# Last-row products in two column halves, activations held to the end of a slot, and projection pieces spread out, in a fused attention and MLP kernel

## The chip, the cores and the metric

The kernel runs on one core of one Trainium2 chip. The metric is the device time of one execution in microseconds (us), as the median of several runs of the same program. The kernel before took 1686.95 us (three runs, 1683.77 to 1687.59). The profiled execution has a span of 1682.0 us from its first to its last instruction, and the traces below count from the start of that span.

A core has five engines that run side by side and meet through semaphores: TensorE (PE in the profile; PEld is its loading of weights), VectorE (DVE), ScalarE (ACT), GpSimd (POOL) and SyncE (SP), which here only issues transfers.

## The reference

Attention that keeps the 32 largest scores of every row, and then a two-layer perceptron with an exact gelu:

```python
# q, k, v: (8 batches, 8 heads, 576 rows, 64), float32
scores = (q @ k.T) / sqrt(64)
kth    = 32nd largest of each row of scores
scores = where(scores >= kth, scores, -1e9)
attn   = exp(scores - rowmax) / (sum + 1e-9)
x      = (attn @ v), heads side by side       # (4608, 512)
out    = gelu(x @ w_in) @ w_out               # (512, 2048), (2048, 512)
```

Everything is float32. TensorE takes each float32 product in two passes, so that the trace has two matmul records for each product in the source; a transpose takes one.

## The kernel before

A batch has 576 rows: 4 blocks of 128 rows (`SM` = 512) and 64 last rows (`TL` = 64). Heads go in pairs. The work is cut into 144 **items**: 128 of them are one block of 128 rows for two heads, and 16 gather the last 64 rows of four heads (two pairs) into one block of 128. A loop over **slots** n issues, for different items, each stage of the attention, and fills in **pieces** of the perceptron. Tile scheduling is manual: every engine runs its instructions in the order in which this program issues them.

```python
for n in range(ahead):                       # one slot
    left[0] = 7 if START < n < START + 2 * NP else 8     # pieces in this slot; START = 10
    weights_add(unit_in(n))
    scores(n + 2)                            # PE, then two ACT copies
    product = attend(n - 3)                  # PE: attn @ v, then ACT copies to xT
    late = n > START + 1
    mlp(1)                                   # one piece: 0.86 us of PE
    tr = transposes(n - 2)                   # [tails, main(0), main(1)]
    ...                                      # (cut: where the next piece needs this product)
    softmax(n - 1, 0)                        # ACT: Prelu, Exp
    mlp(1)
    if not late:
        softmax(n - 1, 1)
    mlp(1)
    for piece in tr[:-1]:
        piece(); ready[0] = n_tok[0]; mlp(1)
    ready[0] = n_tok[0]
    if late:
        softmax(n - 1, 1)
    add_small(n - 1)                         # POOL: den
    for piece in tr[-1:] + prep_in.pop(n, []):   # prep: q and k of a later pair, transposed
        piece(); mlp(1)
    mlp(left[0])
    if n < N:
        top_k(n, {3: lambda: inverse(n - 1)})    # DVE
    threshold(n)                             # POOL
    normalise(n - 1)                         # POOL: two multiplications
    ...                                      # (cut: weights, loads)
```

The product with v for a block of 128 rows (two blocks together, 256 columns) and for last rows:

```python
o = ps.tile([P, 512], f32, tag="tp", name="o")
if t < NM:                                   # 128-row items: a head in each column half
    for j in range(NJ):                      # NJ = 5 blocks of keys
        for e in range(2):
            nc.tensor.matmul(o[e * D : (e + 1) * D, 0:n], lhsT=vt[:, j, e, :],          # L448
                             rhs=pt[:, e * NM + j if j < NM else 2 * NM, :], ...)
    nc.scalar.copy(out=xT[:, at, c], in_=o[:, 0:n])                                     # L453
else:                                        # last rows: both heads of v at once
    for r in range(2):
        vt = raw_of("v", pair + r)
        for j in range(NJ):
            nc.tensor.matmul(o[:, r * P : (r + 1) * P],                                 # L458
                             lhsT=vt[:, j].rearrange("p e d -> p (e d)"),
                             rhs=pt[:, r, j, :], ...)
    for e in range(2):
        r = slice(e * D, (e + 1) * D)
        nc.scalar.copy(out=xT[r, at : at + 2, c], in_=halves(o[r, 0 : 2 * P], e, P))    # L464
```

In the last-row form, 128 columns of v (two heads) meet 128 columns of attention (two heads). Of the four 64 x 64 blocks that come out, the two that join v of one head with the attention of the other are not used.

The scores are products of 64 x 128 parts of the array, or 64 x 64 for last rows (L294: 128 x 64 with 64 moving columns; L305: 64 x 64):

```python
nc.tensor.matmul(t_ps[half(r, e), r * TL : (r + 1) * TL],                               # L294
                 lhsT=qk[:, SM + e * TL : SM + (e + 1) * TL],
                 rhs=qk[:, SM + P + e * TL : SM + P + (e + 1) * TL], ...)
```

The PSUM tag "tp" has two buffers, which the small score tile `t_ps`, the product `o`, the transposes `tp_t` and `tp`, and the projections' transposes `tp_qk` take in turn. Each is freed by an ACT copy.

The perceptron goes in blocks of eight pieces: first layer (L496, into `h_ps`, tag "l1", two buffers), then second layer of the units before (L532). The gelu of two `h_ps` tiles is issued with the sixth piece of a second-layer block:

```python
def gelus(us):
    for u in us:
        g_of[u] = work.tile([P, nf, n], f32, tag="g", bufs=4, name="g")
        nc.scalar.activation(g_of[u], h_of.pop(u), func=AF.Gelu)                        # L507

def behind(work, x, us):                     # x = GELU_AT = 5
    need, f = work[x]
    work[x] = need, lambda: (f(), gelus(us))
    return work
```

Of the kernel before, what the change touches and what calls it, by code (L numbers as in the profile page):

```python
# [14 lines left out]
def kernel(  # L15
# [19 lines left out]
    nc = tc.nc  # L35
# [5 lines left out]
    B, H, S, D = q.shape  # L41
    P = 128
# [6 lines left out]
    TL = S - SM  # L49
    NJ = NM + 1  # L50
# [10 lines left out]
    work = ctx.enter_context(tc.tile_pool(name="work", bufs=2))  # L61
# [6 lines left out]
    xT = const.tile([P, KO, RING], f32, name="xT")  # L68
# [15 lines left out]
    def raw_of(n, pair):  # L84
        return raws[n][pair % len(raws[n])]

    def load(n, pair, queue=None, queue2=None):
        if pair >= n_pairs:
            return
        queue = queue or nc.sync  # L90
        queue2 = queue2 or queue
        b, h0 = pair // NP, 2 * (pair % NP)
        t, src = raw_of(n, pair), sources[n]
        for e in range(2):
            queue.dma_start(
                out=t[:, 0:NM, e, :], in_=src[b, h0 + e, 0:SM].rearrange("(t p) d -> p t d", p=P)
            )
            queue2.dma_start(out=t[e * TL : (e + 1) * TL, NM, e, :], in_=src[b, h0 + e, SM:S])
# [23 lines left out]
    START = 2 * NP + 2  # L122
# [60 lines left out]
    def weights_add(u):  # L183
        if u in words:
            w, _, dst = parts(u)
            d = dst.bitcast(i32)
            if on_pool(u):
                nc.gpsimd.tensor_scalar(
                    w.bitcast(i32), w.bitcast(u32), 2.0**-13, None, op0=ALU.mult
                )  # L190
            nc.gpsimd.tensor_tensor(d, d, w.bitcast(i32), op=ALU.add)
# [23 lines left out]
    def place_of(b, row):  # L215

        if row < SM:
            return b // 2 * RING + b % 2 * (SM + 2 * TL) + row
        return b // 2 * RING + SM + b % 2 * TL + row - SM
# [37 lines left out]
    def spread(t, step, n):  # L257

        return bass.AP(tensor=t.tensor, offset=t.offset, ap=[list(t.ap[0]), [step, 2], [1, n]])

    def half(r, e):


        return slice((r ^ e) * TL, ((r ^ e) + 1) * TL)

    def halves(t, e, step):

        return spread(t[:, e * TL :], step + (TL if e == 0 else -TL), TL)
# [84 lines left out]
    def inverse(i):  # L353
        if i < 0 or i >= N:
            return
        st = stat_of[i]
        nc.vector.reciprocal(st["rden"], st["den"])  # L357

    def add_small(i):
        if i < 0 or i >= N:  # L360
            return
        st = stat_of[i]
        nc.gpsimd.tensor_scalar(st["den"], st["den"], 1e-9, None, op0=ALU.add)  # L363

    def softmax(i, e):

        if i < 0 or i >= N:
            return
        st, s = stat_of[i], row(i, e)
        nc.scalar.activation(s, s, func=AF.Prelu, bias=st["neg"][:, e, 1:2], scale=1.0, alpha=STEEP)  # L370
        nc.scalar.activation(  # L371
            s, s, func=AF.Exp, bias=st["bias"][:, e : e + 1], scale=1.0,
            accum_out=st["den"][:, e : e + 1],
        )
# [55 lines left out]
    def attend(i):  # L430

        if i < 0 or i >= N:
            return False
        pair, t = items[i]
        b, at = divmod(pair, NP)
        if t < NM and t % 2 == 0:
            return False
        pt = pt_now[0]
        o = ps.tile([P, 512], f32, tag="tp", name="o")
        n, row = (2 * P, (t - 1) * P) if t < NM else (TL, SM)  # L440
        tok = place_of(b, row)
        assert read[0] >= tok + n - RING
        c = slice(tok % RING, tok % RING + n)
        if t < NM:
            vt = raw_of("v", pair)
            for j in range(NJ):
                for e in range(2):
                    nc.tensor.matmul(  # L448
                        o[e * D : (e + 1) * D, 0:n], lhsT=vt[:, j, e, :],
                        rhs=pt[:, e * NM + j if j < NM else 2 * NM, :],  # L450
                        start=(j == 0), stop=(j == NJ - 1),
                    )
            nc.scalar.copy(out=xT[:, at, c], in_=o[:, 0:n])  # L453
        else:
            for r in range(2):
                vt = raw_of("v", pair + r)
                for j in range(NJ):
                    nc.tensor.matmul(  # L458
                        o[:, r * P : (r + 1) * P], lhsT=vt[:, j].rearrange("p e d -> p (e d)"),
                        rhs=pt[:, r, j, :], start=(j == 0), stop=(j == NJ - 1),  # L460
                    )
            for e in range(2):
                r = slice(e * D, (e + 1) * D)
                nc.scalar.copy(out=xT[r, at : at + 2, c], in_=halves(o[r, 0 : 2 * P], e, P))  # L464

        if t == (NM if b % 2 == 0 else NM - 1):
            for r in range(2 if t == NM else 1):
                load("v", pair + r + NP + 1)
        if at == (NP - 1 if t < NM else NP - 2):
            assert n_tok[0] == tok  # L470
            n_tok[0] = tok + n
        return True
# [10 lines left out]
    def h_tile(u):  # L483
        if u not in h_of:
            _, n, _, nf = units[u]
            h_of[u] = ps.tile([P, nf, n], f32, tag="l1", name="h_ps")
        return h_of[u]

    def l1_piece(u, x):
        tok, n, f0, nf = units[u]  # L490
        m = 4 // nf
        i, part, c0 = x // m, x % m, tok % RING
        f = f0 + i
        assert all(2 * (f * P // WS) + r in made for r in range(2))
        for ko in range(part * KO // m, (part + 1) * KO // m):
            nc.tensor.matmul(  # L496
                h_tile(u)[:, i, :], lhsT=w_in_sb[:, ko, f * P : (f + 1) * P],
                rhs=xT[:, ko, c0 : c0 + n], start=(ko == 0), stop=(ko == KO - 1),
            )
        if f == FT - 1 and part == m - 1:  # L500
            read[0] = tok + n

    def gelus(us):
        for u in us:
            _, n, _, nf = units[u]
            g_of[u] = work.tile([P, nf, n], f32, tag="g", bufs=4, name="g")
            nc.scalar.activation(g_of[u], h_of.pop(u), func=AF.Gelu)  # L507
# [37 lines left out]
    pieces = []  # L545
    GELU_AT = 5

    def block(u, first):

        do, need = (l1_piece, units[u][0] + units[u][1]) if first else (l2_piece, 0)  # L550
        return [(need, lambda w=w, x=x: do(w, x)) for w in (u, u + 1) for x in range(4)]

    def behind(work, x, us):
        need, f = work[x]
        work[x] = need, lambda: (f(), gelus(us))
        return work

    pieces += behind(block(0, True), 7, (0, 1)) + block(2, True)
    for u in range(2, NU, 2):
# [4 lines left out]
    done = [0]  # L564

    def mlp(n):
        for _ in range(n):
            if done[0] >= len(pieces) or pieces[done[0]][0] > ready[0] or left[0] == 0:
                return
            pieces[done[0]][1]()  # L570
            done[0] += 1
            left[0] -= 1
# [32 lines left out]
    prep_in = {}  # L605
    for pair in range(2, n_pairs):
        b, p = divmod(pair, NP)
# [3 lines left out]
    for n in range(ahead):  # L611

        left[0] = 7 if START < n < START + 2 * NP else 8
        weights_add(unit_in(n))
        scores(n + 2)
        product = attend(n - 3)
        late = n > START + 1
        mlp(1)
        tr = transposes(n - 2)
        if product and n > START and done[0] < len(pieces) and pieces[done[0]][0] > ready[0]:  # L620

            for piece in tr[:1]:
                piece()
            tr, ready[0] = tr[1:], n_tok[0]
        softmax(n - 1, 0)
        mlp(1)
        if not late:
            softmax(n - 1, 1)
        mlp(1)
        for piece in tr[:-1]:  # L630
            piece()
            ready[0] = n_tok[0]
            mlp(1)
        ready[0] = n_tok[0]
        if late:
            softmax(n - 1, 1)
        add_small(n - 1)
        for piece in tr[-1:] + prep_in.pop(n, []):
            piece()
            mlp(1)  # L640
        mlp(left[0])
        if n < N:
            top_k(n, {3: lambda: inverse(n - 1)})
        else:
            inverse(n - 1)
        threshold(n)
        normalise(n - 1)

        weights_sign(unit_in(n))
        weights_size(unit_in(n + 1))  # L650
        if n >= FIRST:
            load_weights(n + 2)
        if n <= NP:
            load("v", n)

    ready[0], left[0] = NT, len(pieces)
    mlp(len(pieces))
    staging.close()


# [30 lines left out]
```

## Time and profile before

| | busy, share of the span | instructions |
|---|---|---|
| PE | 1608.8 us, 96% | 8512 |
| DVE | 1428.6 us, 85% | 3043 |
| ACT | 1189.3 us, 71% | 2147 |
| POOL | 661.9 us, 39% | 761 |

A matmul's end in the trace is modelled, and matmuls overlap, so that the busy share of PE says when it stood idle but not how fast it went. The time that a group of matmuls really takes is the distance from its first start to the start of whatever comes next on PE. ACT loads a table 136 times in all (68 ahead of gelus, 67 ahead of exponentials, one at the start), at 1283 ns each. The waits named below are those that the trace infers from semaphores: "X <- Y" says that X stood idle until Y was done.

### The profile page before, as it was taken

What the parts mean: (1) busy time and instruction counts of PE and PEld (TensorE: products, weight loads), DVE (VectorE), ACT (ScalarE), POOL (GpSimd) and SP (SyncE); (2) the same over time, 40 slices, a digit from 0 to 9 for tenths busy, and PEclk for the clock granted to TensorE, in tenths of its full rate; (3) what the DMA queues carried; (4) which work ended last, traced back from release to release, by engine and by line L of the source; (5) the groups of instructions that cost most, each with busy time, mean ns of one, the idle gap of its engine ahead of it and who ended that gap; (6) DMA issues with size and microseconds to landing.
All of it is one profiled execution on the core that took longest, in us unless ns stands there. A gap on an engine that the chain in (4) does not pass through costs nothing.

```text
span 1682.0 us, 24466 instructions
## 1 busy us (share of the span) xinstructions
PE 1608.8 (96%) x8512; PEld 1095.1 (65%) x8512; DVE 1428.6 (85%) x3043; ACT 1189.3 (71%) x2147; POOL 661.9 (39%) x761
## 2 busy tenths in 40 slices
PE   5559999999999999999999999999999999999999
PEld 4336567766666667676666667676666666766665
DVE  7998988998889888998989888898889998899900
ACT  6887767777777767777777776777777777777730
POOL 3778733333333333333333333333333333333410
PEclk7669999999999999999999999999999999999999
DMA  6422310011100111001100111001110000000000
GB/s 160 136 101 92 91 42 1 13 29 29 44 6 15 29 39 31 1 21 42 29 27 1 42 29 42 1 14 28 36 41 1 27 15 16 20 1 13 7 13 12
DMA packets 126618, 56.10 MB, mean 33 GB/s; under 512 B 117760, under 2 KB 117792, under 8 KB 126496
## 3 DMA queue, kind: packets, MB, share of 16 engines
q1 hardware_dynamic: 125376, 54.25, 11.9%
q8 instruction: 67, 1.10, 0.3%
q14 instruction: 55, 0.45, 0.1%
q10 hardware_dynamic: 1056, 0.26, 0.1%
q0 software_dynamic: 64, 0.03, 0.0%
HBM read 45.08 MB, written 9.44 MB: 32 GB/s over the span
## 4 chain that ended last, share of the span: by engine, by line
PE 88%; DVE 6%; ACT 4%; issue 1%; POOL 1%; ACTq 0%; POOLq 0%
PE h_ps L496 30%; PE y_ps L532 28%; PE o L448 8%; PE s_ps L284 7%; PE tp L417 7%; DVE top L331 3%; DVE rest L334 3%; PE o L458 2%; PE tp_qk L239 2%; PE t_ps L280 2%; PE tp_t L399 1%; PE s_ps L305 1%; ACT s L371 1%; ACT L507 1%; ACT s L370 1%
## 5 line engine op out<-in xcount | busy, mean ns | idle before, releaser
L331 DVE MAX8 top<-rest 128x8 f32<-128x576 f32 x864 | 610.4, 749 | 0.0
L496 PE MATMUL h_ps<-xT,w_in_sb 128*128 128x256 f32 (+1 forms) x2560 | 553.2, 361 | 1.6 <-ACT g L507 1.6
L532 PE MATMUL y_ps<-w_out_sb,g 128*128 128x512 f32 x1152 | 548.6, 598 | 0.0
L382 POOL TENSOR_SCALAR s<-s,rden 128x576 f32<-128x576 f32 x288 | 493.5, 1723 | 1.0 <-issue 0.7
L496 PEld LDWEIGHTS h_ps<-xT,w_in_sb 128*128 128x128 f32 x2560 | 429.4, 191 | 63.7 <-issue 18.4
L334 DVE MATCH_REPLACE8 rest<-top,rest 128x576 f32<-128x576 f32 x576 | 424.0, 745 | 0.0
L363 POOL TENSOR_SCALAR den<-den 128x2 f32<-128x2 f32 x144 | 32.0, 222 | 858.2 <-ACT s L371 857.5
L532 PEld LDWEIGHTS y_ps<-w_out_sb,g 128*128 128x128 f32 x1152 | 195.1, 190 | 166.0 <-issue 164.5
L288 ACT ACTIVATE s<-s_ps 128x1024 f32<-128x1024 f32 x128 | 131.5, 1028 | 170.1 <-PE s_ps L284 149.8
L371 ACT ACTIVATE s<-s,bias 128x576 f32<-128x576 f32 x288 | 223.3, 775 | 13.0 <-ACT s L370 0.4
L370 ACT ACTIVATE s<-s,neg 128x576 f32<-128x576 f32 x288 | 223.7, 777 | 0.8 <-POOL neg L346 0.2
L424 ACT COPY pt<-tp 128x512 f32<-128x512 f32 x256 | 147.1, 575 | 100.6 <-PE tp L417 100.1
L334 DVE MATCH_REPLACE8 rest<-top,s 128x576 f32<-128x576 f32 x288 | 212.0, 745 | 0.0
L417 PEld LDWEIGHTS tp<-ident,s 128*128 128x128 f32 x1152 | 147.8, 145 | 90.5 <-issue 57.5
L331 DVE MAX8 top<-s 128x8 f32<-128x576 f32 x288 | 202.1, 745 | 3.9 <-ACT s L289 3.9
L417 PE MATMUL tp<-ident,s 128*128 128x128 f32 x1152 | 177.7, 279 | 5.8 <-ACT pt L400 5.8
L357 DVE RECIPROCAL rden<-den 128x2 f32<-128x2 f32 x144 | 23.4, 163 | 165.4 <-POOL den L363 165.1
L448 PE MATMUL o<-pt,raw_v 128*64 128x256 f32 x1280 | 156.2, 391 | 1.8 <-ACT pt L424 1.8
L284 PE MATMUL s_ps<-qk 64*128 64x256 f32 x1024 | 152.6, 418 | 0.7 <-ACT s L288 0.7
L448 PEld LDWEIGHTS o<-pt,raw_v 128*64 128x64 f32 x1280 | 87.9, 139 | 69.5 <-issue 16.3
L284 PEld LDWEIGHTS s_ps<-qk 64*128 64x128 f32 x1024 | 92.0, 194 | 23.7 <-issue 1.8
L507 ACT ACTIVATE g<-h_ps 128x512 f32<-128x512 f32 x144 | 78.7, 595 | 39.6 <-PE h_ps L496 38.9
(63 smaller groups left out, 1110.6 us busy)
## 6 DMA issues: line engine op xcount, KB each, us to landing
raw_q<-in_q_dram SPq DMA_DIRECT2D x64, 128.0 KB, 2.3
raw_v<-in_v_dram SPq DMA_DIRECT2D x64, 128.0 KB, 2.4
out_dram<-y SPq DMA_DIRECT2D x32, 256.0 KB, 2.2
w_out_sb<-in_moe_w_in_dram SPq DMA_DIRECT2D x16, 511.8 KB, 4.8
raw_k<-in_k_dram SPq DMA_DIRECT2D x62, 128.0 KB, 2.4
w_out_sb<-in_moe_w_out_dram SPq DMA_DIRECT2D x10, 511.8 KB, 3.7
words<-in_moe_w_out_dram SPq DMA_DIRECT2D x6, 511.8 KB, 4.2
raw_q<-in_q_dram SPq DMA_DIRECT2D x64, 16.0 KB, 2.2
```

The source lines that it names most:

```text
L284: nc.tensor.matmul(s_ps[:, e, c * 256 : (c + 1) * 256], lhsT=lhsT[rows, :], rhs=qk[rows, KT + c * 256 : KT + (c + 1) * 256], start=True, s ...
L288: nc.scalar.activation(spread(s, S + TL, SM), s_ps, func=AF.Copy, scale=scale)
L331: nc.vector.max(st["top"][:, e, 8 * r : 8 * r + 8], cur[e])
L334: nc.vector.match_replace(rest[:, e], st["top"][:, e, 8 * r : 8 * r + 8], cur[e], LOWEST)
L370: nc.scalar.activation(s, s, func=AF.Prelu, bias=st["neg"][:, e, 1:2], scale=1.0, alpha=STEEP)
L371: nc.scalar.activation(s, s, func=AF.Exp, bias=st["bias"][:, e : e + 1], scale=1.0, accum_out=st["den"][:, e : e + 1],)
L382: nc.gpsimd.tensor_scalar(s, s, st["rden"][:, e : e + 1], None, op0=ALU.mult)
L417: nc.tensor.transpose(tp[:, j * P : (j + 1) * P], s[:, first + j * P : first + (j + 1) * P], ident)
L424: nc.scalar.copy(out=dst, in_=tp.rearrange("p (j n) -> p j n", j=NM))
L448: nc.tensor.matmul(o[e * D : (e + 1) * D, 0:n], lhsT=vt[:, j, e, :], rhs=pt[:, e * NM + j if j < NM else 2 * NM, :], start=(j == 0), stop= ...
L496: nc.tensor.matmul(h_tile(u)[:, i, :], lhsT=w_in_sb[:, ko, f * P : (f + 1) * P], rhs=xT[:, ko, c0 : c0 + n], start=(ko == 0), stop=(ko == ...
L532: nc.tensor.matmul(y_of[sub], lhsT=g_of[u][:, i, sub * P : (sub + 1) * P], rhs=w_out_sb[:, f, :], start=(f == 0), stop=(f == FT - 1),)
```

## The change

It has three parts.

1. **Last rows by heads.** Each product of the last rows is cut into two: v of one head (64 columns) with the attention of that head alone (64 columns), in the half of the array's columns and of the PSUM partitions that belongs to this head. The unused blocks are no longer computed, and one ACT copy moves both heads to `xT`.
2. **Gelus held.** A gelu is put on a waiting list when its piece has run, and issued at the end of the slot: after the slot's softmax, copies and preparation, ahead of the last pieces, or earlier if a first-layer block begins and needs the `h_ps` buffer. What it is for: ACT runs its work in order, and other ACT copies for which TensorE waits shall not stand behind a table load and two gelus.
3. **Preparation spread.** In a slot with two groups of preparation, the first one goes between the transposes instead of both going to the end. Besides, the later place of the second softmax half (`late`) begins one slot earlier.

```diff
@@ attend, last rows @@
                 for j in range(NJ):
-                    nc.tensor.matmul(
-                        o[:, r * P : (r + 1) * P], lhsT=vt[:, j].rearrange("p e d -> p (e d)"),
-                        rhs=pt[:, r, j, :], start=(j == 0), stop=(j == NJ - 1),
-                    )
-            for e in range(2):
-                r = slice(e * D, (e + 1) * D)
-                nc.scalar.copy(out=xT[r, at : at + 2, c], in_=halves(o[r, 0 : 2 * P], e, P))
+                    for e in range(2):
+                        nc.tensor.matmul(
+                            o[e * D : (e + 1) * D, r * TL : (r + 1) * TL], lhsT=vt[:, j, e, :],
+                            rhs=pt[:, r, j, half(r, e)], start=(j == 0), stop=(j == NJ - 1),
+                        )
+            nc.scalar.copy(
+                out=xT[:, at : at + 2, c],
+                in_=o[:, 0 : 2 * TL].rearrange("p (r n) -> p r n", r=2),
+            )
@@ l1_piece @@
+        if x == 0:
+            run_gelus()
@@ behind @@
+    waiting = []
     def behind(work, x, us):
         need, f = work[x]
-        work[x] = need, lambda: (f(), gelus(us))
+        work[x] = need, lambda: (f(), waiting.append(us))
         return work
+    def run_gelus():
+        while waiting:
+            gelus(waiting.pop(0))
@@ the loop over slots @@
-        late = n > START + 1
+        late = n > START
 ...
+        prep = prep_in.pop(n, [])
+        if len(prep) > 1 and len(tr) == 3:
+            tr, prep = tr[:1] + prep[:1] + tr[1:], prep[1:]
         for piece in tr[:-1]:
 ...
-        for piece in tr[-1:] + prep_in.pop(n, []):
+        for piece in tr[-1:] + prep:
             piece()
             mlp(1)
+        run_gelus()
         mlp(left[0])
+        run_gelus()
@@ the end @@
-    mlp(len(pieces))
+    while done[0] < len(pieces):
+        mlp(1)
+        run_gelus()
```

## The prediction, made before the changed kernel ran

> **What bounds the kernel now.** I read the page first: the busy shares, and the span in 40 slices.
>
> ```profile
> PE 1608.8 (96%) x8512; PEld 1095.1 (65%) x8512; DVE 1428.6 (85%) x3043; ACT 1189.3 (71%) x2147; POOL 661.9 (39%) x761
> ...
> PE   5559999999999999999999999999999999999999
> ```
>
> PE is below nine tenths in the first three slices only, so the span falls into stages, and I asked for the busy times of each stage (columns: window, length, then PE, PEld, DVE, ACT, POOL, the granted clock, DMA share, GB/s).
>
> ```profile
> 0.00:124.00 124.00, 70.72 (x363) 48.90 (x364) 113.37 (x231) 94.33 (x154) 71.30 (x75) 0.71 0.45 133
> 124.00:210.00 86.00, 79.64 (x434) 52.79 (x433) 79.42 (x162) 68.71 (x116) 69.78 (x49) 0.98 0.29 91
> 210.00:1596.00 1386.00, 1376.15 (x7411) 941.04 (x7412) 1235.68 (x2651) 1008.32 (x1848) 513.44 (x633) 1.00 0.09 22
> 1596.00:1682.00 86.00, 82.32 (x312) 52.33 (x308) 0.17 (x1) 17.92 (x32) 7.34 (x7) 1.00 0.03 13
> ```
>
> Until 124 us DVE is the bound (113.37 of 124 us), and the change hardly touches that. From 210 to 1596 us PE is busy for all but 10 us of 1386, at full clock; the last 86 us are the perceptron alone, again on PE. So whatever shortens PE's own work or its waits after 124 us shortens the time one for one, as long as nothing else takes over. Then the waits of PE in the steady stage (engine, line, what it waited for: us in total, times, longest):
>
> ```profile
> PE t_ps L280 <- ACT qk L243: 3.8, 3, 1.3
> PE t_ps L294 <- ACT qk L243: 2.5, 3, 0.8
> PE o L448 <- ACT pt L424: 1.8, 1, 1.8
> PE t_ps L280 <- ACT pt L424: 1.2, 1, 1.2
> PE tp_t L404 <- POOL s L382: 0.4, 1, 0.4
> ```
>
> All but the last name an ACT copy. The timeline of ACT ahead of one of them shows why the copy was late (start, duration, instruction):
>
> ```profile
> 455.47 0.56 ACT L424 COPY pt<-tp 128x512 f32<-128x512 f32 x1
> 456.04 1.28 ACT L507 ACT_TABLE_LOAD   x1
> 457.34 1.08 ACT L507 ACTIVATE g<-h_ps 128x512 f32<-128x512 f32 x2
> 458.31 0.59 ACT L243 COPY qk<-tp_qk 128x512 f32<-128x512 f32 x1
> ```
>
> The copy of qk stands behind 2.3 us of table load and gelus; PE's next scores start at 458.95, as soon as it is done. What a group of matmuls takes I read as the distance between starts on PE's timeline:
>
> ```profile
> 167.52 0.45 PE L294 MATMUL t_ps<-qk 128*64 128x64 f32 x8
> 167.90 1.09 PE L305 MATMUL s_ps<-qk 64*64 64x512 f32 x8
> ...
> 229.53 2.50 PE L458 MATMUL o<-ptt,raw_v 128*128 128x128 f32 x20
> 231.86 1.02 PE L532 MATMUL y_ps<-w_out_sb,g 128*128 128x512 f32 x2
> ...
> 898.16 2.38 PE L448 MATMUL o<-pt,raw_v 128*64 128x256 f32 x20
> 900.47 0.70 PE L496 MATMUL h_ps<-xT,w_in_sb 128*128 128x256 f32 x2
> ```
>
> A last-row product takes 231.86 - 229.53 = 2.33 us now, and its single records start 111.5 ns apart. L448 does 20 passes of 256 columns in 2.31 us, where 20 full-width passes of 256 columns, as L496 has them, start 216 ns apart and would take 4.32: its two column halves run at the same time.
>
> [...] records of L448 start in pairs 7 ns apart, a pair every 216 ns. [...] from the last pair of L448 to the first L496 it takes 103 ns more than a pair, and the first L496 pass takes 320 instead of 216 ns, together 0.2 us. [...]
>
> **Part 1, last rows by heads.** An item has 2 pairs x 5 blocks x 2 passes = 20 passes of 128 columns, and afterwards 40 of 64 columns on half the array. L294 has exactly that shape (128 rows, 64 weight columns, 64 moving columns): its records start in pairs, a pair every 58 ns, after a first pair of 107 ns. So 20 pairs take 20 x 58 = 1.16 us, plus 0.05 for the first. New is a change of mode on leaving, since now the perceptron follows directly at full width and before it the product was at full width too: 0.2 us, as after L448. The change on entering exists already. Sum 1.16 + 0.05 + 0.2 = 1.42 us (rounded), against 2.33: **0.91 us less for each of 16 items, 14.5 us**, all of it after 210 us, where PE is the bound. The ACT copies go from 32 of 259 ns to 16 of about the same: 4 us less on ACT, which lies beside other work.
>
> **Part 2, gelus held, steady stage.** In the changed order of ACT the copy of qk stands ahead of the gelus in every slot that has both. The six waits of t_ps for qk should go: 3.8 + 2.5 us idle, and about 0.16 us each that the modelled ends of matmuls hide, 1.0 in all. Besides, about 17 products of L448 start some 0.06 us late behind the same copies: 1.0. Together **8.3 us**. What it may cost: gelus end later. In a slot with preparation they start when qk is copied, about 0.9 us before the slot's end by my adding up of eight pieces at 0.86 us, scores of 1.5 and transposes, and so end about 1.5 us into the next slot, just as the next scores (1.5 us of PE) become ready for ACT. The h_ps buffers are needed there only after scores and product, 3.9 us in. So I expect no new wait in the steady stage. The number of table loads stays: gelus were already one batch in a slot.
>
> **Parts 2 and 3 in the ramp (124 to 225 us).** Here slots are short of ready work, and the places shift, in four slots. Slot 11: the copy of tails stood behind both halves of the softmax, and PE waited 2.3 us for it; with the second half later it is 0.97 + 0.78 us earlier: 1.7 gained. Slot 15: gelus now come after tails and preparation, so the first-layer block that waits for h_ps (1.6 us now) starts about 0.8 later, and the second transposes' copy, behind a softmax, comes later too, while a wait of 0.7 us for the second preparation group goes: 1.2 lost. Slot 17: gelus move from the middle to the end, so the main copies come 2.4 us earlier and the waits of 1.2 and 1.8 us at 212 and 215 us go, then 0.4: up to 3.5 gained. Sum 4.0; with normalisation on POOL close behind, I take **3.5**. The spread of preparation in the steady stage moves copies by half a us inside slots and, by the waits above, frees nothing further.
>
> **Sum.** 14.5 + 8.3 + 3.5 = 26.3 us; 1686.95 - 26.3 = 1660.6, so 1661 us, 1.5% less.
>
> **Rivals.** *The halves do not pay.* With 80 loads and matmuls in about 1.2 us, PE's issue of instructions may be the limit; L294 shows the pace for 8 passes only, not for 40. If each pass took 56 ns instead of 29, the product would stay at 2.24 us and lose 0.2 us to the mode: 16 x 0.1 = 2 us lost instead of 14.5 gained, and 1677. Against it: the pairs of L294 hold the same pace up to the last. *Another engine takes over.* DVE needs 9.7 us for an item's top-k without a wait (from 886.33 to 896.03 us), and PE's slots last 11.0 us on average (123 slots from 212 to 1567 us), those with a last-row product 11.7, afterwards 10.8. That stays above DVE, but a chain runs beside it: softmax, denominator, reciprocal after the top-k, 3.43 us of normalisation, then the tails. In one slot that I followed it had 1.3 us to spare; spreading preparation delays the second softmax by about 1.3 us. Where it runs out, a wait for normalisation replaces what was gained, a few us in all: about 1667. *The gelu's wait moves.* If ACT runs later than I count, PE waits for the score tile or for h_ps instead of qk: part 2 gives back up to 8 us, and 1669. *The ramp gives nothing,* or slot 15 costs more than I count: 1664 to 1666.
>
> **Range and chances.** The first rival would show as a whole, but is unlikely; the others are partial. On the other side the ramp may give 3 us more, if everything behind slot 11 moves up. I set 1653 to 1669. Over 2% faster would be below 1653.2: 0.08. Within 2%: 0.91. Slower by over 2%: 0.01.
>
> **What would show it.** Right: the product's line has 640 passes, and start to start an item takes about 1.4 us; no wait of t_ps for qk is left in the steady stage; PE's busy time falls by about 14 us; the last stage of 86 us is unchanged; 68 table loads ahead of gelus, give or take two. Wrong: an item near 2.2 us (issue bound); new lines of PE waiting for POOL's normalisation or for g; at 185 us a longer wait for g than 1.6 us, with more lost than the 1.2 that I set.

## The result, and the profile after

The changed kernel takes **1660.88 us** (median of four runs, 1659.89 to 1662.99) against 1686.57 of the kernel before, a ratio of 0.9852 with a 95% interval of 0.9835 to 0.9869. Runs of one kernel scatter by one to five us, so that step by step I use the profiled executions, which are 1682.0 us before and 1658.1 us after, 23.9 us apart.

The busy times of the page, and of the long stage (window, length, then PE, PEld, DVE, ACT, POOL, clock, DMA share, GB/s):

```profile
PE 1590.1 (96%) x8832; PEld 1079.1 (65%) x8832; DVE 1428.5 (86%) x3043; ACT 1182.8 (71%) x2131; POOL 661.6 (40%) x761
```

```profile
210.00:1596.00 1386.00, 1382.97 (x7859) 942.98 (x7858) 1237.16 (x2656) 1013.34 (x1851) 522.25 (x640) 1.00 0.09 22
```

PE has 320 more instructions and 19 us less busy time. In the long stage it now stands idle for 3 of 1386 us instead of 10. Its waits from 125 us on:

```profile
PE h_ps L500 <- ACT g L511: 3.7, 2, 2.6
PE tp_t L404 <- POOL s L382: 2.9, 2, 1.5
PE tp L417 <- ACT pt L400: 2.0, 2, 1.3
PE tp_t L399 <- POOL s L382: 1.1, 2, 0.6
PE t_ps L294 <- ACT pt L424: 0.9, 2, 0.6
```

The waits of t_ps for qk are gone. All that is left lies in the ramp, but for 1.2 us in the last slot. ACT's timeline at the place that was shown before the change (slot 39) has the new order:

```profile
449.58 0.56 ACT L424 COPY pt<-tp 128x512 f32<-128x512 f32 x1
450.11 0.58 ACT L243 COPY qk<-tp_qk 128x512 f32<-128x512 f32 x1
450.97 0.58 ACT L542 COPY y<-y_ps 128x512 f32<-128x512 f32 x1 [0.28 <-PE y_ps L536]
451.57 1.28 ACT L511 ACT_TABLE_LOAD   x1
```

The copy of qk follows the transposes' copy at once; PE's next scores start at 451.63, unhindered. And a last-row product on PE's timeline:

```profile
227.66 1.39 PE L459 MATMUL o<-ptt,raw_v 128*64 128x64 f32 x40
228.98 2.84 PE L536 MATMUL y_ps<-w_out_sb,g 128*128 128x512 f32 x6
```

Start to start it is 1.32 us for 40 passes, where 20 full-width passes took 2.33.

The starts of the scores bound each slot. Their distances, in us, say where the 23.9 us came from:

| | before | after | gained |
|---|---|---|---|
| start of the first scores | 9.0 | 9.4 | -0.4 |
| slot 11 | 13.13 | 9.85 | 3.3 |
| slot 14 | 11.58 | 11.99 | -0.4 |
| slot 15 | 12.45 | 15.39 | -2.9 |
| slot 16 | 11.59 | 11.78 | -0.2 |
| slots 17 and 18 | 9.03 + 15.98 | 7.64 + 14.92 | 2.4 |
| 16 slots with a last-row product | 11.68 (first of them) | 10.76 | 14.7 |
| the other slots from 23 to 140 | | | 8.8 |
| from slot 141's scores to the end | 114.6 | 116.0 | -1.45 |

### The profile page after: what moved, and what is told of

The parts are those of the page before. It is cut to its first block, busy times and chain, and to the rows that moved or that the text cites. A ratio compares the mean times of both kernels' runs of the same rounds, so it can differ in the third digit from the quotient of the medians.

```text
span 1658.1 us, 25071 instructions
## 1 busy us (share of the span) xinstructions
PE 1590.1 (96%) x8832; PEld 1079.1 (65%) x8832; DVE 1428.5 (86%) x3043; ACT 1182.8 (71%) x2131; POOL 661.6 (40%) x761
## 4 chain that ended last, share of the span: by engine, by line
PE 89%; DVE 6%; ACT 2%; POOL 1%; issue 1%; POOLq 0%; ACTq 0%
PE h_ps L500 30%; PE y_ps L536 29%; PE o L448 8%; PE s_ps L284 7%; PE tp L417 7%; DVE top L331 3%; DVE rest L334 3%; PE tp_qk L239 2%; PE t_ps L280 2%; PE o L459 1%; PE tp_t L399 1%; PE s_ps L305 1%; POOL s L382 1%; DVE w_in_sb L199 0%; ACT s L371 0%
## 5 line engine op out<-in xcount | busy, mean ns | idle before, releaser
L448 PE MATMUL o<-pt,raw_v 128*64 128x256 f32 x1280 | 155.1, 389 | 0.0
L448 PEld LDWEIGHTS o<-pt,raw_v 128*64 128x64 f32 x1280 | 87.5, 139 | 65.8 <-issue 23.9
```

## The experiments

Ten kernels ran. "Span" is that of the profiled execution. They ran in three groups, each beside the kernel before, whose median in them was 1684.45 to 1686.89 us; differences of two or three us between rows are therefore read from the spans and slots. The diffs are abridged where `...` stands.

| kernel | median us | ratio to before, 95% interval | span us |
|---|---|---|---|
| part 1 alone | 1669.31 | 0.9908, 0.9895 to 0.9921 | 1667.0 |
| part 2 alone | 1673.97 | 0.9935, 0.9923 to 0.9947 | 1672.0 |
| part 3 alone | 1693.86 | 1.0052, 1.0039 to 1.0065 | 1689.3 |
| parts 1 and 2 | 1659.56 | 0.9850, 0.9837 to 0.9864 | 1657.7 |
| changed, halves in turn | 1672.0 | 0.9915, 0.9900 to 0.9929 | 1670.3 |
| changed, a piece between | 1669.41 | 0.9898, 0.9883 to 0.9913 | 1667.7 |
| changed, one block of five | 1647.83 | 0.9772, 0.9756 to 0.9788 | 1646.3 |
| changed, with the rule | 1657.4 | 0.9833, 0.9820 to 0.9846 | 1655.4 |
| parts 1, 2, the rule | 1657.4 | 0.9838, 0.9825 to 0.9852 | 1655.0 |
| parts 1, 2, the rule, late from slot 11 | 1654.3 | 0.9819, 0.9806 to 0.9833 | 1652.9 |

**Part 1 alone.**

```diff
-                    nc.tensor.matmul(o[:, r * P : (r + 1) * P], lhsT=<both heads>, rhs=pt[:, r, j, :])
+                    for e in range(2):
+                        nc.tensor.matmul(o[e * D : (e + 1) * D, r * TL : (r + 1) * TL],
+                                         lhsT=vt[:, j, e, :], rhs=pt[:, r, j, half(r, e)])
...                                      # (cut: start and stop; the copies change as shown above)
```

> The kernel before with part 1 alone (last-row products by heads). If TensorE bounds the steady stage and nothing takes over: an item takes 1.42 us instead of 2.33, 16 items, so 14.6 us less, about 1672 us, and slots with a last-row product fall from 11.7 to 10.8 us. If another engine or the normalisation chain takes over behind it: less than 10 us gained, 1677 or more, with new waits of TensorE for POOL's normalisation.

The span fell by 15.0 us; by the medians it is 17.1. Slots with a last-row product take 10.69 to 10.80 us, as in the changed kernel, and PE's waits in the steady stage are those of before (3.8 and 2.5 us for qk). Nothing takes over: the first theory.

**Part 2 alone.**

```diff
-        work[x] = need, lambda: (f(), gelus(us))
+        work[x] = need, lambda: (f(), waiting.append(us))
...
+        run_gelus()
         mlp(left[0])
```

> The kernel before with part 2 alone (gelus held). Theory: the waits of scores for the qk copy go in the steady stage (8.3 us by the prediction, 8.8 by the changed kernel's slots), slot 17 gains about 3, slot 15 loses about 1, and the last slot loses 1.3 because its gelus now wait for the end of a second-layer block: 9.5 us in all, about 1677 us. Rival, the wait only moves to h_ps or to the score tile: under 4 us gained, 1683 or more.

The median fell by 12.4 us, the span by 10.0. From slot 23 to slot 141 it gained 8.8 us (1283.8 against 1292.6); slots 17 and 18 gained 3.4; slot 15 lost 0.3; the end lost 1.45. From 230 us to the last slot no wait of PE is left. The wait does not move: it goes.

**Part 3 alone.**

```diff
-        late = n > START + 1
+        late = n > START
+        prep = prep_in.pop(n, [])
+        if len(prep) > 1 and len(tr) == 3:
+            tr, prep = tr[:1] + prep[:1] + tr[1:], prep[1:]
```

> The kernel before with part 3 alone (preparation spread, second softmax half late one slot earlier). Theory: slot 11 gains the 3.3 us that it gained in the changed kernel, the steady stage nothing: 1683 us. Rival: the gain of slot 11 is taken back at the normalisation of the next slots, or the spread makes new waits: 1686 to 1687.

It was slower by 7.5 us, which neither expectation had. Slot 11 did gain 3.3. But from slot 23 to slot 141 the kernel took 1302.0 us instead of 1292.6, and the first line of PE's waits from 125 us on was new:

```profile
PE t_ps L294 <- ACT pt L424: 10.5, 5, 2.9
```

ACT's and PE's timelines show it (once in each odd batch, 2.93 us long in three of the four):

```profile
584.49 1.28 ACT L507 ACT_TABLE_LOAD   x1
585.78 1.09 ACT L507 ACTIVATE g<-h_ps 128x512 f32<-128x512 f32 x2
586.75 0.78 ACT L370 ACTIVATE s<-s,neg 128x576 f32<-128x576 f32 x1
587.55 1.28 ACT L371 ACT_TABLE_LOAD   x1
...
589.62 0.56 ACT L424 COPY pt<-tp 128x512 f32<-128x512 f32 x1
```

```profile
590.23 0.45 PE L294 MATMUL t_ps<-qk 128*64 128x64 f32 x8 [2.93 <-ACT pt L424]
```

A preparation group between the transposes brings the sixth piece of the second-layer block, and with it the gelus, ahead of the second half of the softmax and of the second transposes' copy. These then stand behind two table loads, and with them the buffer that the next scores need. The 9.4 us are made of three slots that take 2.1 us longer and, in the slots behind two of them, 1.6 us more at half of TensorE's clock. With gelus held no such wait is left after the ramp: part 3 is harmful without part 2.

**Parts 1 and 2 without part 3.** The edit is the two diffs above together.

> The kernel before with parts 1 and 2, without part 3. If parts 1 and 2 carry the whole gain and the spread only undoes in slot 15 what it brings in slot 11: as fast as the changed kernel or up to 1 us faster, 1660 to 1661 us, with the scores of slot 19 starting at about 225.5 us as with part 2 alone. If part 3 adds to the others (the parts alone give 17.1, 12.4 and minus 7.5 us, which sums to 22, and the whole gave 25.7): 3 us or more slower than the changed kernel, 1664 us.

It is as fast as the changed kernel (ratio 0.9850 against 0.9852). From slot 23 to slot 141 both take 1272.8 us, so that in the steady stage the spread is worth nothing. In the ramp slot 11 lacks its 3.3 us (13.11), while slot 15 takes 12.76 instead of 15.39, though PE waits 2.57 us for g there too, and slot 18 takes 13.97 instead of 14.92. Scores of slot 19 start at 225.9 us, and at 226.3 us in the changed kernel.

**Halves in turn.**

```diff
-                for j in range(NJ):
-                    for e in range(2):
+                for e in range(2):
+                    for j in range(NJ):
                         nc.tensor.matmul(o[e * D : (e + 1) * D, r * TL : (r + 1) * TL], ...)
```

> The changed kernel, but all five products of one head ahead of the five of the other, so that neighbours use the same half of the columns. Same instructions, same number of mode changes. If the gain of part 1 comes from two halves running at the same time, which needs neighbours in different halves: an item goes to about 40 x 56 ns + 0.25 = 2.5 us, 1.1 us more for each of 16 items, about 1678 us. If a 64-column pass is cheap in itself (29 ns each): no change, 1661 us.

```profile
229.88 2.01 PE L459 MATMUL o<-ptt,raw_v 128*64 128x64 f32 x40
231.81 1.55 PE L536 MATMUL y_ps<-w_out_sb,g 128*128 128x512 f32 x3
```

An item takes 1.94 us instead of 1.32, 0.62 more, and the kernel is 11.1 us slower: 10.0 in the slots with a last-row product, and most of the rest at half clock in slot 18 (16.25 us, against 14.92). So it is the overlap of two halves that pays. A step takes 58 ns in both kernels, but an item has 20 steps of two passes in the changed kernel and 31 here. The size I expected (2.5 us) was too large: 9 of the 40 records start only 3 to 6 ns after the one before, so some overlap remains although neighbours in the program use the same half. How PE comes to it I did not settle.

**A piece between.**

```diff
             for r in range(2):
                 vt = raw_of("v", pair + r)
+                if r == 1:
+                    mlp(1)
```

> The changed kernel, but with one of the slot's perceptron pieces moved between the two pairs of a last-row product, which adds a change of tiling mode in each direction and no work. If leaving the half-width mode costs 0.2 us and entering it 0.1: 0.3 us for each of 16 items, 5 us, about 1666 us. If a change of mode costs nothing and what was seen after L448 belongs to that line alone: 1661 us.

```profile
231.06 0.80 PE L461 MATMUL o<-ptt,raw_v 128*64 128x64 f32 x20
231.79 1.12 PE L538 MATMUL y_ps<-w_out_sb,g 128*128 128x512 f32 x2
232.85 0.80 PE L461 MATMUL o<-ptt,raw_v 128*64 128x64 f32 x20
233.58 1.13 PE L538 MATMUL y_ps<-w_out_sb,g 128*128 128x512 f32 x2
```

The piece takes 1.06 us between the halves, against 0.86 elsewhere, and each half 0.73. Of the first four slots with a last-row product, three are 0.35 us longer than in the changed kernel and one 0.50. A change from half width to full and back thus costs about 0.35 us, near the 0.3 expected, which makes 6 us of the 8.5 by which this kernel is slower. Most of the rest is one slot of the ramp, slot 18 (17.83 us, against 14.92), whose instructions are the same in both kernels: in this profile PE has half its clock for 6.8 us there, and in the changed kernel's not at all.

**One block of five.** This kernel leaves out four of the five blocks of keys in the last-row products, and its output lacks them.

```diff
-                for j in range(NJ):
+                for j in range(1):
...                                      # (cut: stop=(j == 0))
```

> The changed kernel with four of the five blocks of keys left out of the last-row products (the output is no longer the reference's): 8 passes instead of 40, by 4 pairs of 58 ns + 0.25 = 0.48 us an item, 0.93 less than now. If TensorE still bounds the slots with last-row products at 9.8 us: 14.9 us less, about 1646 us. If the top-k of 9.7 us with its chain through normalisation takes over before: 1652 us or more, with TensorE waiting for POOL.

The last-row slots take 9.83 us (10.03 and 9.76 for two of them), as expected for a product of 0.48 us, and PE has no wait in them. The median is 13.1 us below the changed kernel's; 14.3 of it are in the steady slots (one of each four saves 0.77 instead of 0.93), and slot 19 begins 2.5 us later, again for the clock in slot 18. So at slots of 9.8 us DVE's 9.7 us of top-k still does not take over, at least not in the four such slots that follow one another.

**With the rule.** Gelus are issued at once where the next first-layer block begins in the same slot, and in the last slot.

```diff
+    def at_once(x):
+        nxt = done[0] + 8 - x
+        fits = left[0] > 8 - x and nxt < len(pieces) and pieces[nxt][0] <= n_tok[0]
+        return fits or slot[0] >= ahead - 1
...                                      # (cut: slot[0] is set to n in the loop over slots)
-        work[x] = need, lambda: (f(), waiting.append(us))
+        work[x] = need, lambda: (f(), waiting.append(us), at_once(x) and run_gelus())
```

> The changed kernel, but gelus are issued at once where the next first-layer block begins in the same slot (that is slot 15 alone), and in the last slot. If holding the gelus is what made slot 15 take 15.4 us instead of 12.5 and the end wait 1.3 us: 4 us less than the changed kernel, about 1657 us. Rival, slot 15 lost its time to the spread preparation: only the 1.3 us of the end come back, 1659.5 us.

1657.4 us, 3.5 less. Slot 15 is back at 12.76 us, and the end at 114.6. But slot 18 grew to 16.58, so that scores of slot 19 start only 1.2 us earlier. PE waits there for normalisation as in the changed kernel (2.9 us in two waits). From this I took slot 18 to be bound by normalisation on POOL whatever comes ahead of it, and tested that with the next two.

**The rule without part 3, and with the late softmax alone.** The first is parts 1 and 2 with the rule; the second adds one line:

```diff
-        late = n > START + 1
+        late = n > START
```

> Parts 1 and 2 with the rule that issues gelus at once where the next first-layer block begins in the same slot, and in the last slot; no part 3. If slot 18 is bound by normalisation on POOL behind the top-k, what slots 11 to 17 gain before it is lost there: the same as the second version with part 3, 1657 to 1658 us, 1.4 us of it against parts 1 and 2 alone from the last slot. If the ramp adds up slot by slot: 3 us slower, 1660.5 us, for want of slot 11's gain.

> As the run before, and with the second half of the softmax late from slot 11 on, which is part 3 without the spread. If slot 18 is bound by normalisation: 1657 to 1658 us again. If the ramp adds up: 1657 us from slot 11's 3.3 us, against 1660.5 without.

They took 1657.4 and **1654.3 us**. The first number would fit the theory, the second does not, and slot 18 contradicts it in both: 13.97 and 14.00 us, although in the second it starts as early (208.5 us) as in the version with the spread, where it took 16.58. The spread makes the smaller part of this difference. In slot 16 it sends the second half of the softmax later: the denominator reaches POOL 11.4 us after the slot's start in the changed kernel (203.28 us) and 10.3 us in the last version (199.50). On POOL, behind it, stand a normalisation, a weight conversion of 5.4 us and the next normalisation back to back, for which slot 18 waits: 2.9 us with the spread; without it 1.2, and 0.9 for a copy of scores on ACT. That is 0.9 us less, as much as lies between 14.92 us in the changed kernel and 14.00 here. The other 1.7 of the 16.58 us are a stretch of 3.4 us at half clock, from 216.0 us on. The changed kernel has the same 2.9 us of waits and no such stretch; the next section shows what differs between the two. None of the four kernels that hold gelus and leave out the spread has one there, and in the last version what slot 11 gains stays to the end. It is the fastest: 6.6 us below the changed kernel by the medians, 5.2 by the spans. Two of PE's waits in it from 125 us on:

```profile
PE h_ps L500 <- ACT g L511: 1.6, 1, 1.6
PE tp_t L404 <- POOL s L382: 1.2, 1, 1.2
```

The 1.2 us of the last slot are gone, and slot 15's wait for g is 1.6 us instead of 2.6.

## Why the prediction was right, and where it was not

The predicted 1661 us is within 0.2 us of the median. By its steps:

- **PE bounds, one for one: right.** What PE was spared came back in full in the part 1 run (0.92 us in each of 16 slots), and all but 0.6 of 14.9 us in the run with one block of five.
- **Part 1, 14.5 us: right.** An item takes 1.32 us to the next start, and the first full-width pass behind it 0.10 more, 1.42 in all as predicted. The slots measure 0.92 us for the predicted 0.91. The pace of L294's four pairs held for twenty (a pair every 58 to 59 ns), and the mode change cost what L448 had shown. PE's busy time fell by 19 us where 14 were named as a sign; as the ends of matmuls are modelled it is not a measure of the gain, and the 5 us more are not explained.
- **Part 2 in the steady stage, 8.3 us: right.** 8.8 in the changed kernel and alone.
- **The ramp, 3.5 us: terms mis-sized, 2.2 measured, and most of that by the clock.** The prediction counted PE's waits alone. In slots 11 to 18 they add up to 9.7 us before and 9.5 after. Slot 11 was spared 1.6 us of them (1.7 predicted) and slot 15 got 1.3 more (1.2 predicted). But slots 17 and 18 were spared 0.5 instead of 3.5: the waits for copies went, and 2.9 us of waiting for normalisation on POOL, 0.4 before, took their place. Without the spread (part 2 alone) they were spared 1.4. What the sum lacked is the clock. Before, two waits of the ramp are followed by 3.4 us at half speed, in slots 11 and 18; after, only one, in slot 15. Such a stretch costs about 1.6 us, as two slots of the part 3 run show below. PE's windows of the kernel before (length, PE busy, granted clock, DMA share, GB/s) show the first:

```profile
137.50:140.70 3.20, 0.95 (x5) 1.00 0.71 289
140.70:144.10 3.40, 3.37 (x12) 0.53 0.02 5
```

  With the wait of 2.3 us down to 0.7 this stretch went too, and slot 11 gained 3.3. Slots 17 and 18 gained 2.4, most of it by the stretch that they no longer have. Slot 15 went the other way and lost 2.9. There the preparation's copy now stands ahead of the gelus for which the first layer waits:

```profile
185.50 1.58 PE L500 MATMUL h_ps<-xT,w_in_sb 128*128 128x256 f32 x4 [2.57 <-ACT g L511]
```

  With part 2 alone, and with parts 1 and 2, PE waits the same 2.57 us, the clock stays whole, and the slot loses 0.3; so the length of the wait alone does not decide it. What the traces show is where the stretches lie: in the kernel before and in the changed kernel those of the ramp last 3.41 us each, and all stretches of one execution start whole multiples of 3413.3 ns apart, to within 0.01 us (before, 140.88 and 215.97 us, 22 such steps; after, 18.78 and 186.04 us, 49). So a grid of 3.41 us can be laid over each trace, and I call one step of it a window. In the changed kernel the wait, from 182.93 to 185.50 us, lies whole in one window, and the next is at half speed:

```profile
182.62:186.04 3.42, 0.85 (x6) 1.00 0.37 84
186.04:189.45 3.41, 3.41 (x12) 0.50 0.39 89
```

  With part 2 alone the end of a window cuts the wait into 0.87 and 1.70 us, and with parts 1 and 2 into 1.13 and 1.44. Part 3 alone has both cases in one execution. Its wait of 2.93 us lies whole in a window in slots 87 and 123, and each time the next slot takes 1.6 us longer; in slot 51 it is cut, and the next slot takes no longer (the wait of slot 87, then that of slot 51):

```profile
984.85:988.27 3.42, 0.49 (x9) 1.00 0.19 44
988.27:991.68 3.41, 3.41 (x22) 0.50 0.00 0
```

```profile
585.49:588.91 3.42, 1.81 (x8) 1.00 0.43 96
588.91:592.32 3.41, 2.09 (x22) 1.00 0.00 0
```

  From 125 us to the window in which PE's work ends, PE stood idle for 2.29 and 1.77 us of a full-speed window in the trace before and for 2.57 us of one in the trace after, and each time half speed followed; in no other full-speed window of these two was it idle for more than 1.59 us, and behind none of them did it follow. (The ends of matmuls are modelled, so that these are numbers of the records.) Why it follows is not shown. Where the windows lie against the kernel's start differs between the two profiled executions: one begins 0.93 us behind the start of the span before, and 1.72 us after. That the first has two stretches in the ramp and the second has one can therefore be luck in part.
- **The last stage unchanged: wrong, 1.45 us lost.** The last slot has a whole second-layer block at its end, and its gelus now wait until the slot is over. The first layer then waits for them:

```profile
1605.97 2.21 PE L500 MATMUL h_ps<-xT,w_in_sb 128*128 128x256 f32 x9 [1.18 <-ACT g L511]
```

- **The spread frees nothing in the steady stage: right** (1272.8 us with and without). That it would be harmful but for part 2 the prediction did not see.
- **The rivals.** The halves pay. The steady wait did not move to h_ps. Another engine took over in the ramp only, by way of POOL: 2.9 us in slot 18, which took back most of what slots 17 and 18 were to gain, and 1.1 in two slots before.
- **The sum.** 26.3 us predicted, 25.7 by the medians, but 23.9 by the spans on which the steps were built. The two steps that failed both went one way (1.3 and 1.45 us), the start was 0.4 later, and the first would have failed by about 3 us without the clock. That the median hit is thus partly the scatter of the runs and the place of these windows.

## What to carry to other kernels

Where a matmul's output has blocks that nobody reads, try cutting it by column halves and issuing the halves in turns: here an item went from 2.33 to 1.32 us, and the gain could be read ahead from another line of the same shape in the same trace, with 0.2 us for the change of mode behind L448 (in the run with a piece between, one change in and out cost 0.35 us). An instruction for which a whole queue waits (here 2.3 us of a table load with two gelus) belongs behind the copies that free buffers, but ahead of the work that needs its result in the same slot, and a fixed place at the end of the slot fails exactly where that need falls inside. Two moves in one queue are not additive: here part 3 cost 7.5 us alone, and the best version does without its spread. And where a trace shows stretches at half clock, count a wait of about two us with up to 1.7 us behind it (1.6 behind the waits of 2.93 us in slots 87 and 123, 1.7 in slot 18 with the rule), and compare two traces slot by slot only with the half-speed stretches of both beside them.

## What the runs showed that I had not expected

With all products of one half issued ahead of the other's, 9 of 40 passes still started 3 to 6 ns behind the one before, and the item took 1.94 us instead of the 2.3 that 40 steps of 58 ns would make. And the same wait on PE can cost 1.3 to 1.7 us more behind it, or nothing, by where it falls in these windows: in slot 18, four kernels with the same instructions up to there took 14.92 us (no stretch at half clock), 16.25 and 16.31 (one), and 17.83 (two). In the first, waits of 1.54 and 1.41 us lie in two windows; in the others one window holds 2.06 to 2.36 us of them.
